# An attention and feed-forward kernel on one core: two PSUM banks joined wherever they lie, summary products on quadrants, a new table of due times, and identity matmuls ahead of the first chunk

## The chip, the core and the metric

One NeuronCore of a Trainium2 chip. Five engines work on separate instruction streams: PE (TensorE, matmuls; its weight loads are listed as PEld), DVE (VectorE), ACT (ScalarE), POOL (GpSimd) and SP, which here only issues DMAs. Matmuls write to PSUM, eight banks of 512 fp32 per partition; DVE and ACT read PSUM, and all but PE write SBUF. The metric is the device time of one execution in microseconds, the median of three runs.

## What is computed

```python
def mab(q, kv):                       # x: 4 x 12480 x 128, inducing: 32 x 128
    s = scale * (q @ kv.transpose(0, 2, 1))
    s = s - s.max(-1, keepdims=True)
    a = np.exp(s)
    a /= a.sum(-1, keepdims=True) + 1e-09
    return a @ kv
h = mab(I, x)                         # 32 summary rows for each batch
y = mab(x, h)                         # each row of x attends to them
g = where(y @ w_in >= 1, y @ w_in, where(y @ w_in <= -1, 0, (y @ w_in + 1) ** 2 / 4))
out = g @ w_out                       # w_in 128 x 2048, w_out 2048 x 128
```

## The kernel before

The four batches are cut into 26 chunks of 480 rows, 104 chunks in all. A batch has three stages. `summarize` reads x twice over (as rows and as columns), and makes the 32 summary rows h; a chain of small steps c1 to c12 joins its seven groups of four chunks and ends in hT, the transposed summary. `attend`, once for a group of four chunks, turns a chunk's scores against h into weights `a`, splits them into a high part `ahi` and a rest, and sends both by DMA into `aT`. `chunk` is the feed-forward part, and most of the time: since a chunk's attended rows are `a` times h, `y @ w_in` is `aT` times (h times w_in), and that summary product is kept for a batch in the four tiles `hw`, each with h times w_in four times over (two copies of the high part and two of the rest, to go with the four quarters of `aT`).

A chunk has eight steps k, each with two of the 16 blocks of 128 hidden columns. In a step:

- PE: two `hidden` matmuls (L774), each into a PSUM bank of its own, from a pool `h` of seven banks;
- ACT: relu of h + 1 out of PSUM into `w` (L782), then the square of half of it in place (L768);
- DVE: `bound`, min(square, max(h, 1)), out of PSUM and `w` (L787), which frees the banks;
- for six of eight steps (`SPLIT`) a high part `hi` is rounded off, on DVE (L810), ACT (L807) or POOL (L805), as the planner picks; POOL subtracts it (`lo`, L813); and PE adds three products into the chunk's accumulator bank (pool `o`, one bank): w_lo x hi, w_hi x hi, w_hi x lo (L844). In the two other steps PE multiplies `w` itself in full fp32 (L844, `w_f`);
- after eight steps DVE transposes the accumulator (L854), and SP stores it in four DMAs.

Relu and bound of a step are written as one instruction over both banks (128x960) where the second bank is the neighbour of the first and the pair starts on an even bank (`beside`, L83), and as two of 128x480 otherwise.

The order of everything is made ahead of time. `Plan.order` is a list scheduler: it goes through time with a cost and a lag for each operation, and at each moment an engine takes, of the operations whose inputs and buffers are there, the one with the earliest due time. Due times are a step's number times 1950 plus an offset by its kind (`BEHIND`), and offsets of the attention's steps (`STEPS`, `LEAD`, `SC`, `GA`). What it puts out is one fixed stream for each engine; on the chip an engine takes its stream strictly in that order.

The opening: the first summary needs all of batch 0, and the weights arrive as 64-bit numbers that DVE turns into fp32 in six to seven small instructions a tile. PE has no chunk work until hT, hw and the first `aT` are there.

Of the kernel before, what the change touches and what calls it, by code (L numbers as in the profile page):

```python
# [17 lines left out]
SPLIT = (0, 1, 3, 4, 6, 7)  # L18

SLOTS = dict(  # L20
    h=7, o=1, xn=9, xT=26, xr=2, e1=1, eN=1, hw=6, w=8, hi=4, lo=4, aT=3, s2=2, a=1, ahi=1, oT=1
# [3 lines left out]
BEHIND = {  # L25
    "h": -4400, "r": -3050, "s": -700, "t": 400, "hi": 3700, "hi ACT": 14900, "hi POOL": 9600,
    "lo": 2200, "p": 9300, "ps": 8900,
}

LEAD = 66950  # L30
STEPS = [0, 1200, 2400, 3600, 8000, 12000, 13000, 18000, 24000, 28000, 32000]

SC = [0, 1200, 2400]
GA = [0, 1500, 6000, 7500]


# [3 lines left out]

KEEP = 0


class Slot:


    def __init__(self, pool, turn=None, near=None):
        self.pool, self.left, self.until, self.place, self.tile = pool, 0, 0, None, None
        self.turn, self.near, self.first = turn, near, False
        if near:  # L50
            near.first = True

    def pick(self, spare, now):

        free = {i for t, i in spare if t <= now}
        if self.near and self.near.place is not None and self.near.place ^ 1 in free:
            return self.near.place ^ 1
        if self.first:
            return min(free, key=lambda i: (i ^ 1 not in free, i % 2, i))
        return min(free, key=lambda i: (i ^ 1 in free, i))  # L60


class Op:


    def __init__(self, engine, cost, lag, due, emit, needs, uses, tiled):
        choice = engine if isinstance(engine, dict) else {engine: (cost, lag, due)}
        self.choice, self.emit, self.uses = choice, emit, uses
        self.engine, self.cost, self.due = None, 0, due
        self.tiled, self.twin, self.merged, self.wide = tiled, None, None, False  # L70
        self.start = self.after = 0
        self.by = {}
        self.unmet, self.then = 0, []
        for n in needs:
            n.then.append(self)
            self.unmet += 1
        for s in self.uses:
            s.left += 1

    def ready(self, engine):  # L80
        return max([self.after, *(t for e, t in self.by.items() if e == engine)])

    def beside(self):  # L83

        a, b = self.uses[0].place, self.twin.uses[0].place
        return a % 2 == 0 and b == a + 1


class Plan:
# [5 lines left out]
    def add(self, engine, cost, lag, due, emit, needs=(), uses=(), tiled=False):  # L95
        op = Op(engine, cost, lag, due, emit, [n for n in needs if n], uses, tiled)
        self.ops.append(op)
        return op

    @staticmethod  # L100
    def twins(a, b, cost, lag):

        a.twin, b.twin, a.merged = b, a, (cost, lag)

    def order(self):
        engines = sorted({e for op in self.ops for e in op.choice})
        free = dict.fromkeys(engines, 0)
        able = {e: [] for e in engines}

# [3 lines left out]

        for op in self.ops:
            if not op.unmet:
                enable(op)
        spare = {p: [(0, i) for i in range(n)] for p, n in SLOTS.items()}
        turn = dict.fromkeys(SLOTS, 0)
        tiled = False
        now, done = 0, []  # L120
        while len(done) < len(self.ops):
            later = []
            took = False
            for e in engines:
# [3 lines left out]
                best, rank = None, 0  # L128
                for op in able[e]:
# [12 lines left out]
                    due = op.choice[e][2] - (KEEP if e == "PE" and op.tiled == tiled else 0)  # L142
                    if best is None or due < rank:
                        best, rank = op, due
# [6 lines left out]
                for s in best.uses:  # L151
                    if s.place is None:
                        s.place = s.pick(spare[s.pool], now)
# [10 lines left out]
                if e == "PE" and best.tiled != tiled:  # L164
                    cost, lag, tiled = cost + RETILE, lag + RETILE, best.tiled
                for op in both:
                    op.start, op.engine, op.cost, op.lag = now, e, 0, lag
                    done.append(op)
                best.cost = cost
                free[e] = now + cost  # L170
                later.append(free[e])
                for s in [s for op in both for s in op.uses]:
                    s.left -= 1
                    s.until = max(s.until, now + lag)
                    if not s.left:
                        spare[s.pool].append((s.until, s.place))
                for n in [n for op in both for n in op.then]:
                    n.unmet -= 1
                    if list(n.choice) == [e]:
                        n.after = max(n.after, now + cost + RAW[e])  # L180
                    elif e in n.choice:
                        for x in n.choice:
                            n.by[x] = max(n.by.get(x, 0), now + cost + RAW[e] if x == e else now + lag)
                    else:
                        n.after = max(n.after, now + lag)
                    if not n.unmet:
                        enable(n)
# [7 lines left out]
def attn_moe(  # L195
# [38 lines left out]
        xr=([C, NB, M], F32), e1=([P, CW], F32), eN=([96, 5, P], F32), hw=([P, 512], F32R),  # L234
# [23 lines left out]

    turns = dict.fromkeys(SLOTS, 0)

    def in_turn(pool, near=None):
        turns[pool] += 1
        return Slot(pool, turns[pool] - 1, near)
# [127 lines left out]
    def load_out(k, when, due):  # L391
        src = w_out[k * WS : (k + 1) * WS].rearrange("(p t) d -> p t d", t=2)
        if k not in SPLIT:
            w_f[k] = const.tile([P, 2, C], F32, name=f"w_f{k}")
            w_made[k] = load_f32(src, when, due, w_f[k])[0]
            return
        made, f = load_f32(src, when, due)
        w_hi[k] = const.tile([P, 2, C], F32R, name=f"w_hi{k}")
        w_lo[k] = const.tile([P, 2, C], F32R, name=f"w_lo{k}")
        by = lambda a: a.rearrange("p (t c) -> p t c", t=2)  # L400
# [5 lines left out]
        w_made[k] = add("POOL", 650, 750, due, lower, [made], [f])  # L406
# [6 lines left out]
    def summarize(b, begin, pace, end):  # L413
# [7 lines left out]
        def load(g, due, step):  # L421
            for q in range(nqs[g]):
# [6 lines left out]
                    "SP", 700 if b else 960, 3000, due,  # L429
# [20 lines left out]
                else:  # L450
# [6 lines left out]
                    def turn(c=c, xr=xr):  # L457
# [3 lines left out]
                        add("SP", 640, 3200, due - 4000, lambda k=k, fetch=fetch: fetch(k), [], [xr, xT[b, c]])  # L461
                        for k in range(Q)
                    ]
                    xT_made[b, c] = add("DVE", 597, 735, due, turn, l, [xT[b, c], xr])

        def score(g, due):
# [31 lines left out]
            m = add("PE", 850, 1050, due, scores, [ind_made, *(xT_made[b, c] for c in cs)],  # L498
                    [p1, e1[g], *(xT[b, c] for c in cs)], tiled=True)
            v = add("DVE", 760, 900, due + SC[1], most, [m, folded, prior], [p1])  # L500
            return add("ACT", 640, 780, due + SC[2], exps, [v], [e1[g], p1])

        def gather(g, due, scored):
# [32 lines left out]
            def keep():  # L536
                nc.scalar.copy(hs[:rows, g, :], ph.tile[:rows, :C])

            m = add("PE", 110 * T, 110 * T + 200, due, turn, [scored], [*to, e1[g], eN[g]])
            by = dict(ACT=(660, 800, due + GA[1])) if b == 0 else dict(  # L540
                DVE=(598, 740, due + GA[1]), ACT=(503, 640, due + GA[1]))
            v = add(by, 0, 0, 0, put, [m], [eN[g], *to])
            m = add("PE", 220 * T, 220 * T + 200, due + GA[2], weigh, [v],
                    [ph, eN[g], *(xn[g * Q + q] for q in range(nq))], tiled=True)
            lasts.append(add("ACT", 160, 300, due + GA[3], keep, [m, folded, prior], [ph]))
# [66 lines left out]
        def c12():  # L612
            hT[b] = const.tile([C, Q, M], F32, name=f"hT_{b}")
            nc.vector.tensor_copy(hT[b], s_h.tile[:, :M].unsqueeze(1).to_broadcast([C, Q, M]))
# [3 lines left out]
        o = add("DVE", 200, 350, end, c3, [o], [s_m])  # L618
# [8 lines left out]
        hT_made[b] = add("DVE", 180, 320, end, c12, [o], [s_h])  # L627
        hw[b], hw_made[b] = [], []
        for k in range(FF // 512):
            s_w, dst = Slot("h"), Slot("hw")  # L630
            hw[b].append(dst)

            def multiply(k=k, s_w=s_w):
                nc.tensor.matmul(  # L634
                    make(s_w), hT[b].rearrange("c q m -> c (q m)"),
                    w_in_sb[:, k * 512 : (k + 1) * 512], start=True, stop=True,
                )

            def upper(s_w=s_w, dst=dst):
                nc.scalar.copy(make(dst), s_w.tile)  # L640

            def lower(s_w=s_w, dst=dst):
                half = slice(P // 2, P)
                nc.vector.tensor_sub(dst.tile[half], s_w.tile[half], dst.tile[half].bitcast(F32))

            m = add("PE", 860, 1050, end + 1 + 2 * k, multiply, [hT_made[b], *in_made[2 * k : 2 * k + 2]], [s_w, dst])
            c = add("ACT", 485, 620, end + 1 + 2 * k, upper, [m], [dst, s_w])
            hw_made[b].append(add("DVE", 610, 745, end + 2 + 2 * k, lower, [c], [s_w, dst]))
# [4 lines left out]
    def attend(b, g, due):  # L653

        hasty = (b, g) == (0, 0)
        AT = [0] * 11 if hasty else STEPS
# [9 lines left out]
        def scores():  # L666
            p = make(p2)
            for q, c in enumerate(cs):
                nc.tensor.matmul(  # L669
                    p[q * M : (q + 1) * M, :CW], hT[b][:, 0, :], xT[b, c].tile, start=True, stop=True  # L670
# [43 lines left out]
        o = add("PE", 850, 1050, due, scores, [hT_made[b], *(xT_made[b, c] for c in cs)],  # L714
                [p2, p3, s2, *(xT[b, c] for c in cs)], tiled=True)
        o = add("DVE", 600, 740, due + AT[1], turn, [o], [p2, p3])
        o = add("DVE", 562, 700, due + AT[2], most, [o], [p3])
# [197 lines left out]
```

## Time and profile before

| what | us |
|---|---|
| runs, median (lowest to highest) | 1773.66 (1773.36 to 1774.67) |
| the profiled execution | 1771.55 |
| its span, first to last instruction | 1769.7 |
| busy: PE, ACT, DVE, POOL | 1717.7, 1695.4, 1622.8, 1610.4 |
| first `hidden` matmul | 72.06 |

The page gives busy times; groups of instructions by line and by shape give how many there are and how long one takes; the timeline gives starts, and from start to start, where an engine doesn't wait, the step of one. The step is shorter than the duration on PE and ACT, since the next instruction begins before the last has ended: a sum over durations counts too much, and a sum over steps is the load.

### The profile page before, as it was taken

The numbers are of one execution on the slowest core, as the hardware profiler recorded it, in microseconds if no ns is written. First come the engines' busy times: TensorE is split into PE (matmuls) and PEld (weight loads), VectorE is DVE, ScalarE is ACT, GpSimd is POOL, SyncE is SP. The second block draws the span as 40 slices with busy tenths as digits, with TensorE's granted clock in tenths as the row PEclk, the third lists the DMA queues.
The fourth block names the chain that finished last, engine by engine and source line by source line (L and its number), as shares of the span: only waits on it lengthen the run. The fifth ranks groups of instructions, "written<-read, shape, count | busy, mean of one in ns | idle before, by whom it ended". The sixth has DMA issues, their size and how long they took to land.

```text
span 1769.7 us, 26019 instructions
## 1 busy us (share of the span) xinstructions
PE 1717.7 (97%) x7898; PEld 1226.7 (69%) x7898; DVE 1622.8 (92%) x2393; ACT 1695.4 (96%) x2658; POOL 1610.4 (91%) x863
## 2 busy tenths in 40 slices
PE   7699999999999999999999999999999999999998
PEld 5467677777767677776767777677776777777676
DVE  7899889998899898999889999899889999999996
ACT  5599999999999999999999999999999999999997
POOL 0499999999899999999999999999998999999997
PEclk9699999999999999999999999999999999999999
DMA  9532423423232343332233423332211111111111
GB/s 243 98 63 56 79 49 60 72 58 60 44 67 49 62 79 59 65 76 48 47 56 61 72 49 64 70 65 51 45 20 38 34 27 30 35 34 34 33 29 17
DMA packets 425069, 101.78 MB, mean 58 GB/s; under 512 B 369602, under 2 KB 420386, under 8 KB 424930
## 3 DMA queue, kind: packets, MB, share of 16 engines
q1 hardware_dynamic: 424834, 100.01, 30.1%
q8 instruction: 62, 1.02, 0.2%
q14 instruction: 77, 0.63, 0.1%
q10 hardware_dynamic: 96, 0.12, 0.0%
HBM read 48.94 MB, written 25.56 MB: 42 GB/s over the span
## 4 chain that ended last, share of the span: by engine, by line
PE 49%; ACT 25%; DVE 13%; issue 7%; POOL 3%; DMA 2%; SPq 1%; DVEq 0%; POOLq 0%; ACTq 0%
PE banks L844 34%; ACT w L782 13%; PE banks L774 10%; ACT w L768 10%; DVE w L787 7%; DVE hi L810 3%; POOL lo L813 2%; ACT hi L807 1%; PE banks L669 1%; DVE oT L854 1%; PE banks L477 1%; PE banks L530 1%; PE banks L634 1%; SPq L455 1%; POOL hi L805 1%
## 5 line engine op out<-in xcount | busy, mean ns | idle before, releaser
L813 POOL TENSOR_TENSOR lo<-w,hi 128x960 fp32r<-128x960 f32 x624 | 1399.7, 2269 | 63.4 <-DVE hi L810 28.4
L787 DVE SCALAR_TENSOR_TENSOR w<-banks,w 128x480 f32<-128x480 f32 (+1 forms) x1428 | 978.0, 729 | 95.5 <-ACT w L768 85.3
L782 ACT ACTIVATE w<-banks 128x480 f32<-128x480 f32 (+1 forms) x1503 | 889.2, 666 | 12.3 <-PE banks L774 9.5
L768 ACT ACTIVATE w<-w 128x960 f32<-128x960 f32 x832 | 867.0, 1066 | 2.2
L774 PE MATMUL banks<-aT,hw 128*128 128x480 f32 x1664 | 594.9, 431 | 18.2 <-DVE w L787 9.9
L844 PE MATMUL banks<-hi,w_lo 128*128 128x480 f32 x1248 | 538.3, 431 | 9.5 <-DVE oT L854 5.7
L844 PE MATMUL banks<-lo,w_hi 128*128 128x480 f32 x1248 | 474.6, 380 | 1.4 <-POOL lo L813 1.4
L844 PE MATMUL banks<-hi,w_hi 128*128 128x480 f32 x1248 | 474.0, 380 | 0.0
L810 DVE TENSOR_REDUCE hi<-w 128x960 fp32r<-128x960 f32 x373 | 423.7, 1140 | 11.7 <-PE banks L844 0.9
L774 PEld LDWEIGHTS banks<-aT,hw 128*128 128x128 f32 x1664 | 306.7, 189 | 184.1 <-DVE w L787 107.1
L844 PE MATMUL banks<-w,w_f 128*128 128x480 f32 x832 | 393.1, 567 | 0.2 <-DVE oT L854 0.2
L844 PEld LDWEIGHTS banks<-hi,w_lo 128*128 128x128 f32 x1248 | 234.9, 188 | 119.9 <-issue 53.4
L844 PEld LDWEIGHTS banks<-hi,w_hi 128*128 128x128 f32 x1248 | 235.3, 189 | 57.6 <-issue 28.9
L844 PEld LDWEIGHTS banks<-lo,w_hi 128*128 128x128 f32 x1248 | 234.5, 188 | 39.6 <-POOL lo L813 2.9
L844 PEld LDWEIGHTS banks<-w,w_f 128*128 128x128 f32 x832 | 156.1, 189 | 62.6 <-issue 44.3
L805 POOL TENSOR_SCALAR hi<-w 128x960 fp32r<-128x960 f32 x145 | 144.4, 999 | 16.3 <-DVE w L787 9.7
L807 ACT CAST hi<-w 128x960 fp32r<-128x960 f32 x106 | 109.6, 1034 | 7.2 <-PE banks L844 3.3
L854 DVE STREAM_TRANSPOSE oT<-banks 128x480 f32<-128x480 f32 x104 | 70.1, 674 | 7.8 <-PE banks L844 7.5
L403 POOL TENSOR_TENSOR w_lo<-hi,w_hi 128x256 fp32r<-128x256 f32 x6 | 6.5, 1076 | 60.6 <-ACT w_hi L405 60.6
L458 DVE STREAM_TRANSPOSE xT<-xr 128x480 f32<-128x480 f32 x78 | 51.2, 663 | 3.1 <-DMA xr<-in_x 3.0
L712 POOL TENSOR_TENSOR a<-a,ahi 128x480 fp32r<-128x480 f32 (+1 forms) x27 | 33.2, 1231 | 1.3 <-ACT ahi L709 1.3
L530 PE MATMUL banks<-xn,eN 120*32 120x128 f32 (+1 forms) x774 | 31.7, 275 | 0.5 <-ACT eN L522 0.5
(82 smaller groups left out, 553.1 us busy)
## 6 DMA issues: line engine op xcount, KB each, us to landing
out<-oT SPq DMA_DIRECT2D x416, 60.0 KB, 2.2
xn<-in_x SPq DMA_DIRECT2D x93, 240.0 KB, 4.2
xr<-in_x SPq DMA_DIRECT2D x312, 60.0 KB, 2.5
aT<-ahi SPq DMA_DIRECT2D x208, 60.0 KB, 2.0
aT<-a SPq DMA_DIRECT2D x206, 60.0 KB, 2.0
w<-in_x SPq DMA_DIRECT2D x11, 240.0 KB, 4.5
w<-in_moe_w_in SPq DMA_DIRECT2D x8, 256.0 KB, 4.5
w<-in_moe_w_out SPq DMA_DIRECT2D x8, 256.0 KB, 5.3
```

The costliest lines, as they stand in the source:

```text
L458: nc.vector.transpose(make(xT[b, c]), xr.tile.rearrange("c n i -> c (n i)"))
L530: nc.tensor.matmul(p[q * M : (q + 1) * M, :C], eN[g].tile[:, t, q * M : (q + 1) * M], xn[g * Q + q].tile[:, t, :], start=(t == 0), stop=(t ...
L768: nc.scalar.activation(w.tile, w.tile, AF.Square, scale=0.5)
L774: nc.tensor.matmul(make(h)[:, :CW], hw[b][ft // 4].tile[:, ft % 4 * P : (ft % 4 + 1) * P], aT[b, c].tile, start=True, stop=True,)
L782: each(of, i, hs_, w, lambda to, h: nc.scalar.activation(to, h, AF.Relu, bias=1.0))
L787: lambda to, h: nc.vector.scalar_tensor_tensor(to, h, 1.0, to, op0=ALU.max, op1=ALU.min),
L805: nc.gpsimd.tensor_scalar(make(hi), w.tile, 1.0, 0.0, op0=ALU.mult, op1=ALU.add)
L807: nc.scalar.copy(make(hi), w.tile)
L810: nc.vector.tensor_reduce(make(hi), w.tile.unsqueeze(3), axis=AX.X, op=ALU.max)
L813: nc.gpsimd.tensor_sub(make(lo), w.tile, hi.tile.bitcast(F32))
L844: nc.tensor.matmul(acc.tile[:, :CW], wt, g, start=(first and n == 0), stop=(last and n == len(terms) - 1),)
L854: nc.vector.transpose(make(oT).rearrange("c n i -> c (n i)"), acc.tile[:, :CW])
```

## The change

**Joined banks.** `beside` and the rules that looked for neighbouring banks go. Any two banks of a step are read as one operand, with the distance between them as the stride; where the lower bank was taken second, the two halves of the step are swapped (`half`). Relu and bound are joined whenever both halves are ready at once.

**Summary products.** hT is kept once and not four times. The four products h times w_in go side by side into one bank, on the array's four quadrants of 32 columns; ACT rounds them once (`hx`), DVE subtracts once (`hy`), and SP copies 32-row pieces into the four `hw` tiles: 16 DMAs a batch, which weren't there.

**Three products in two parts.** w_lo x hi and w_hi x hi are one operation (`p`), which needs `hi` alone; w_hi x lo is another (`pl`), which needs `lo`.

**Due times.** `BEHIND`, `STEPS`, `LEAD`, `SC` and `GA` give way to a table `DUE` with an offset for each kind and each k. PE gains a bonus of 450 for staying in its mode of tiling, single halves a lateness (`LONE`), and a few costs change by some ns (hi on POOL from 1085 to 1000).

**Identity matmuls.** Up to 180 multiplications of the 128x128 identity by itself stand open to PE, one each 250 ns of the plan from 28 us on, behind everything else and dropped after 2 us; 111 get into the stream. They write the accumulator's bank, which the first chunk gets after them. The copy of the two fp32 weight tiles moves from DVE to ACT.

```diff
-    def beside(self):
-
-        a, b = self.uses[0].place, self.twin.uses[0].place
-        return a % 2 == 0 and b == a + 1
...
-                if best.merged and best.beside():
+                if best.merged:
...
+            a, b = sorted(h.place for h in hs_)
+            do(w.tile, banks[:, a : b + 1 : b - a, :CW])
...
+            for k in range(FF // 512):
+                nc.tensor.matmul(
+                    p[k * M : (k + 1) * M], hT[b], w_in_sb[:, k * 512 : (k + 1) * 512], start=True, stop=True
+                )
...
+                src = (wide_hi if r < 2 else wide_lo).tile[k * M : (k + 1) * M]
+                nc.sync.dma_start((dst.tile or make(dst))[r * M : (r + 1) * M].bitcast(F32), src.bitcast(F32))
...
+                parts = [
+                    ([(w_lo, hi), (w_hi, hi)], 436, "p", [u], [hi]),
+                    ([(w_hi, lo)], 218, "pl", [l], [lo]),
+                ]
...
-BEHIND = {
-    "h": -4400, "r": -3050, "s": -700, "t": 400, "hi": 3700, "hi ACT": 14900, "hi POOL": 9600,
+    "h": [-8100, -3450, -2750, -3300, -3950, 1600, -30300, -35450],
+    "r": [5450, 8600, 10700, -1550, 18200, -11550, -13450, -10800],
...
+    idle = Slot("o")
+
+    def keep_on():
+        nc.tensor.matmul((idle.tile or make(idle))[:, :P], ident, ident, start=True, stop=True)
+
+    for n in range(WARM[1]):
+        begin = WARM[0] + 250 * n
+        add("PE", 215, 415, -EARLY * 1e6 + n, keep_on, [id_made], [idle], span=(begin, begin + 2000))
```

How often each form stands in the streams, counted over all rows of the order:

| form | before | after |
|---|---|---|
| ACT relu, 128x480 / 128x960 | 1342 / 161 | 680 / 492 |
| DVE bound, 128x480 / 128x960 | 1192 / 236 | 0 / 832 |
| hi on DVE / ACT / POOL | 373 / 106 / 145 | 416 / 74 / 134 |
| summary product: PE / ACT / DVE / SP | 16 / 16 / 16 / 0 | 16 (four at once) / 4 / 4 / 64 |
| eN copies of 120 rows: DVE / ACT | 11 / 10 | 4 / 17 |
| identity matmuls | 0 | 111 |

First place: PE between the summary and the first chunk. L634 (before) is a summary product, L669 a chunk's scores against h, L774 a `hidden` matmul. Before:

```order
L634 MATMUL banks<-w_in_sb,hT_906 128x512 x4
L669 MATMUL banks<-xT_298,hT_906 32x480
L669 MATMUL banks<-xT_311,hT_906 32x480
L669 MATMUL banks<-xT_321,hT_906 32x480
L669 MATMUL banks<-xT_359,hT_906 32x480
L669 MATMUL banks<-xT_387,hT_906 32x480
L669 MATMUL banks<-xT_403,hT_906 32x480
L669 MATMUL banks<-xT_413,hT_906 32x480
L669 MATMUL banks<-xT_432,hT_906 32x480
L774 MATMUL banks<-aT_973,hw_925 128x480 x4
```

And now (L654 the product, L701 the scores, L903 the identity, L811 a `hidden` matmul):

```order
L654 MATMUL banks<-w_in_sb,hT_946 32x512 x4
L701 MATMUL banks<-xT_298,hT_946 32x480
L701 MATMUL banks<-xT_311,hT_946 32x480
L701 MATMUL banks<-xT_321,hT_946 32x480
L701 MATMUL banks<-xT_359,hT_946 32x480
L903 MATMUL banks<-ident 128x128 x27
L701 MATMUL banks<-xT_387,hT_946 32x480
L701 MATMUL banks<-xT_403,hT_946 32x480
L701 MATMUL banks<-xT_413,hT_946 32x480
L701 MATMUL banks<-xT_432,hT_946 32x480
L903 MATMUL banks<-ident 128x128 x17
L811 MATMUL banks<-aT_1047,hw_983 128x480 x4
```

Of the 111 identity matmuls 44 stand here, 40 ahead of it among c1 to c12 and the last groups, and 27 between the first chunk's `hidden` matmuls.

Second place: DVE near the end, L787 and L824 the bound, L810 and L847 hi. Before:

```order
L787 SCALAR_TENSOR_TENSOR w_16671<-banks,w_16671 128x480 x2
L787 SCALAR_TENSOR_TENSOR w_16685<-banks,w_16685 128x960
L810 TENSOR_REDUCE hi_16733<-w_16671 128x960
L787 SCALAR_TENSOR_TENSOR w_16700<-banks,w_16700 128x480 x2
L787 SCALAR_TENSOR_TENSOR w_16720<-banks,w_16720 128x480 x2
```

And now:

```order
L824 SCALAR_TENSOR_TENSOR w_15974<-banks,w_15974 128x960
L847 TENSOR_REDUCE hi_16000<-w_15950 128x960
L824 SCALAR_TENSOR_TENSOR w_15979<-banks,w_15979 128x960
L847 TENSOR_REDUCE hi_16021<-w_15979 128x960
L824 SCALAR_TENSOR_TENSOR w_15993<-banks,w_15993 128x960
```

Every bound is one instruction. Third place: PE in a middle chunk, L844 and L876 the products into the accumulator. Before:

```order
L844 MATMUL banks<-hi_7621,w_lo_101 128x480
L844 MATMUL banks<-hi_7621,w_hi_100 128x480
L844 MATMUL banks<-lo_7638,w_hi_100 128x480
L844 MATMUL banks<-hi_7621,w_lo_101 128x480
L844 MATMUL banks<-hi_7621,w_hi_100 128x480
L844 MATMUL banks<-lo_7638,w_hi_100 128x480
L774 MATMUL banks<-aT_7264,hw_4985 128x480 x4
```

And now:

```order
L876 MATMUL banks<-hi_7853,w_lo_91 128x480
L876 MATMUL banks<-hi_7853,w_hi_90 128x480
L876 MATMUL banks<-hi_7853,w_lo_91 128x480
L876 MATMUL banks<-hi_7853,w_hi_90 128x480
L811 MATMUL banks<-aT_7503,hw_4875 128x480
L876 MATMUL banks<-lo_7884,w_hi_90 128x480 x2
```

The products with `lo` come after those with `hi`, and `hidden` matmuls stand between them. At the three later changes of batch the summary product stands 20 to 24 `hidden` matmuls ahead of the first that needs it (before: 16).

More of the change, by code (lines that the diff above doesn't have):

```diff
@@ L108, in order @@
         able = {e: [] for e in engines}
+        spare = {p: [(0, i) for i in range(n)] for p, n in SLOTS.items()}
+        turn = dict.fromkeys(SLOTS, 0)
+        tiled = False
+        now, done, left = 0, [], len(self.ops)
         def enable(op):
@@ L116, in order @@
                 enable(op)
[L117 to L121, printed above, removed]
+        while left:
             later = []
@@ L168, in order @@
                     done.append(op)
+                    left -= 1
+                    finish(op, e, cost, lag)
                 best.cost = cost
[L170 to L187, printed above, removed]
             if not took:
```

285 lines of the change are left out of this document (152 added, 133 removed), and 15 rows, old and new, of the table DUE.

## The prediction

> **What bounds the kernel now.** I read the page's busy times first, then a table of windows, then groups of instructions by shape, and last the timeline of three engines for their steps. A difference of 0.2% (3.5 us) is about what a measurement of this kernel can tell from none. The page, and the engines' busy time in a quiet stretch (length, then PE, PEld, DVE, ACT, POOL in us with counts, PE's granted clock, DMA):
>
> ```profile
> PE 1717.7 (97%) x7898; PEld 1226.7 (69%) x7898; DVE 1622.8 (92%) x2393; ACT 1695.4 (96%) x2658; POOL 1610.4 (91%) x863
> 300.00:400.00 100.00, 99.43 (x473) 71.72 (x472) 94.18 (x141) 99.86 (x161) 96.29 (x51) 1.00 0.34 63
> ```
>
> Four engines are nearly full at once, so the question is whose load is largest. Busy time overstates it for ACT and PE, whose instructions overlap, so I count instructions and multiply by steps, start to start. The groups (count, busy us and mean ns, idle before):
>
> ```profile
> L813 POOL TENSOR_TENSOR lo<-w,hi 128x960 fp32r<-128x960 f32 x624 | 1399.7, 2269 | 63.4 <-DVE hi L810 28.4 <-ACT hi L807 8.5 <-PE banks L844 7.4
> L768 ACT ACTIVATE w<-w 128x960 f32<-128x960 f32 x832 | 867.0, 1066 | 2.2
> L782 ACT ACTIVATE w<-banks 128x480 f32<-128x480 f32 x1342 | 733.4, 626 | 11.5 <-PE banks L774 8.7 <-DMA aT<-a 1.2
> L787 DVE SCALAR_TENSOR_TENSOR w<-banks,w 128x480 f32<-128x480 f32 x1192 | 713.9, 645 | 45.2 <-ACT w L768 41.7 <-POOL lo L813 1.7
> L810 DVE TENSOR_REDUCE hi<-w 128x960 fp32r<-128x960 f32 x373 | 423.7, 1140 | 11.7 <-PE banks L844 0.9 <-POOL hi L805 0.5
> L787 DVE SCALAR_TENSOR_TENSOR w<-banks,w 128x960 f32<-128x960 f32 x236 | 269.2, 1149 | 50.3 <-ACT w L768 43.6 <-issue 3.8 <-POOL hi L805 1.6
> L782 ACT ACTIVATE w<-banks 128x960 f32<-128x960 f32 x161 | 160.8, 1002 | 0.8 <-PE banks L774 0.8
> L805 POOL TENSOR_SCALAR hi<-w 128x960 fp32r<-128x960 f32 x145 | 144.4, 999 | 16.3 <-DVE w L787 9.7 <-PE banks L844 1.3 <-DVE sm L698 1.1
> L807 ACT CAST hi<-w 128x960 fp32r<-128x960 f32 x106 | 109.6, 1034 | 7.2 <-PE banks L844 3.3 <-DVE w L787 2.7 <-DVE nm L585 0.6
> L644 DVE TENSOR_TENSOR hw<-banks,hw 64x512 fp32r<-64x512 f32 x16 | 10.9, 693 | 3.7 <-ACT hw L640 3.3
> ```
>
> Steps on ACT (start, duration, row), all without a wait:
>
> ```profile
> 1743.73 0.99 ACT L782 ACTIVATE w<-banks 128x960 f32<-128x960 f32 x1
> 1744.58 1.02 ACT L807 CAST hi<-w 128x960 fp32r<-128x960 f32 x1
> 1745.46 1.07 ACT L782 ACTIVATE w<-banks 128x480 f32<-128x480 f32 x2
> 1746.37 1.05 ACT L768 ACTIVATE w<-w 128x960 f32<-128x960 f32 x1
> 1747.27 1.07 ACT L782 ACTIVATE w<-banks 128x480 f32<-128x480 f32 x2
> ```
>
> A joined relu takes 0.85 us, a pair of single ones 0.91, a cast 0.88, a square 0.90. On DVE:
>
> ```profile
> 1717.71 1.14 DVE L810 TENSOR_REDUCE hi<-w 128x960 fp32r<-128x960 f32 x1
> 1718.77 1.15 DVE L787 SCALAR_TENSOR_TENSOR w<-banks,w 128x960 f32<-128x960 f32 x1
> 1719.83 0.67 DVE L854 STREAM_TRANSPOSE oT<-banks 128x480 f32<-128x480 f32 x1
> 1720.43 1.19 DVE L787 SCALAR_TENSOR_TENSOR w<-banks,w 128x480 f32<-128x480 f32 x2
> 1721.53 1.14 DVE L810 TENSOR_REDUCE hi<-w 128x960 fp32r<-128x960 f32 x1
> ```
>
> Joined bound 1.06, pair 1.10, hi 1.06. On PE, an fp32r matmul steps (1760.86 - 1758.91) / 9 = 0.217 us over the rows below, and the two full fp32 ones (four records) take 1758.91 - 0.22 - 1757.09 = 1.60, so 0.80 each:
>
> ```profile
> 1757.09 1.77 PE L844 MATMUL banks<-w,w_f 128*128 128x480 f32 x4
> 1758.32 0.75 PE L844 MATMUL banks<-hi,w_lo 128*128 128x480 f32 x1
> 1758.91 0.38 PE L844 MATMUL banks<-hi,w_hi 128*128 128x480 f32 x1
> ...
> 1760.86 0.38 PE L844 MATMUL banks<-hi,w_hi 128*128 128x480 f32 x1
> ```
>
> Loads in the chunk stage, which I take from the first `hidden` matmul at 72.06 (quoted below) to the end of the span, 1769.7, so 1698 us. ACT: 671 pairs x 0.91 + 161 x 0.85 + 832 x 0.90 + 106 x 0.88 = 1590, and some 55 of attention steps, an estimate from four kinds of 21 to 28 of about half a us: 1645, or 96.9% of the stage. PE: 1664 + 3 x 1248 = 5408 matmuls x 0.217 = 1173, 416 x 0.80 = 333, some 104 of attention and summary, an estimate: 1610, 94.8%. POOL: 1610 busy, of which an estimated 9 lie before the stage: 1601, 94.3%. DVE: 596 pairs x 1.10 + 236 x 1.06 + 373 x 1.06 = 1301, and some 224 of transposes and attention, an estimate: 1525, 90%. So ACT is the bound, by a small lead, and the waits agree:
>
> ```profile
> ACT w L782 <- PE banks L774: 9.5, 17, 1.5
> DVE w L787 <- ACT w L768: 85.3, 124, 2.9
> PE banks L774 <- DVE w L787: 9.9, 21, 1.4
> ```
>
> DVE waits for ACT's square, ACT hardly for anyone.
>
> **The change: ACT.** By the counts in the order, 331 steps more have a joined relu: 331 x (0.91 - 0.85) = 20 us less. 32 casts go: 32 x 0.88 = 28 less. Nine summary casts fewer and seven eN copies more cancel. ACT: 1645 - 48 = 1597. No row shows a pair of banks that are not neighbours. If its access costs as two singles, the 20 us stay; that it costs less than neighbours I exclude, as it is the same form with a longer stride. I take the neighbours' 0.85, the nearest row.
>
> **DVE, POOL, PE.** DVE: 596 more joined bounds x 0.04 = 24 less, 43 more hi x 1.06 = 46 more, 9 summary subtractions and 7 copies of about 0.6 less, 10: 1525 + 12 = 1537, still the lightest. POOL: 11 hi of 1.0 less: 1590. PE: 12 products in the stage are about 0.86 each when the clock is full (512/480 of 0.80); three joint ones replace them. On quadrants the nearest rows are the scores (0.85 for four, below); dearer than 0.9 or cheaper than 0.8 moves the sum by 0.3 us. So 7.6 less: 1602. Cutting the products with `lo` apart adds no matmul. It takes PE's wait for POOL off the products with `hi`, which I cost at nothing: the waits that PE shows there come to a few us.
>
> The largest load falls from 1645 to 1602, and now three engines lie within 12 us of each other. If the top one keeps nearly the share that ACT has, 96.7% for 96.9, the stage takes 1602 / 0.967 = 1657: **41 us less**.
>
> **The 64 new DMAs.** The nearest rows are the aT load's, from SP too (the page's, with the us to landing, and two issues in the timeline):
>
> ```profile
> aT<-ahi SPq DMA_DIRECT2D x208, 60.0 KB, 2.0
> 72.24 1.22 SPq L733 DMA_DIRECT2D aT<-ahi  x2
> ```
>
> Sixteen at a change of batch, at about 0.6 us of issue, are 10 us, and 2.0 to land. Behind them on SP stand aT loads and stores. In the order the product stands 20 to 24 `hidden` matmuls ahead of its first use, that is 1.25 chunks or more, and a chunk takes 1698 / 104 = 16 us: 20 us cover 13. If that cover is gone, it costs up to 10 us at each of three changes. I take nothing.
>
> **The opening.** The clock (column after the five engines) and PE's rows:
>
> ```profile
> 50.00:53.00 3.00, 0.71 (x4) 0.62 (x3) 2.88 (x13) 0.67 (x2) 0.38 (x2) 0.50 1.14 222
> 53.00:56.00 3.00, 3.00 (x14) 2.94 (x14) 2.17 (x7) 0.00 (x0) 0.75 (x1) 0.50 0.84 122
> 68.00:70.00 2.00, 0.00 (x0) 0.00 (x0) 1.98 (x4) 0.44 (x1) 0.00 (x0) 0.81 0.12 30
> 52.88 3.20 PE L610 MATMUL banks<-ff,hs 128*128 128x32 f32 x14 [1.13 <-DVE ff L602]
> 56.46 1.83 PE L669 MATMUL banks<-xT,hT 128*32 128x480 f32 x8 [0.38 <-DVE hT L614]
> 58.22 5.78 PE L634 MATMUL banks<-w_in_sb,hT 128*128 128x512 f32 x8
> 63.93 1.01 PE L669 MATMUL banks<-xT,hT 128*32 128x480 f32 x8
> 72.06 1.17 PE L774 MATMUL banks<-aT,hw 128*128 128x480 f32 x2 [5.09 <-DMA aT<-a]
> ```
>
> At half clock the same scores take 1.83 us that take 1.01 at full. With the clock held, c11 (L610) saves 3.20 x (1 - 1.01 / 1.83) = 1.4 and the first scores 0.8. On DVE one summary subtraction stands between the scores and aT where three of 0.69 did: 1.4. The identity matmuls, 0.80 x 128/480 = 0.21 us each, an estimate from the fp32 step, hide in PE's waits; the six or seven ahead of c4, c8 and c11 fill those waits a little more than full, 0.4 late in all. 27 + 17 between the scores are 9.4 us beside the chain of some 12 on DVE. Together 3.2 us earlier. After 72 ACT was full anyway, so a warm clock there is worth nothing more.
>
> By the Trainium skill's page "TensorE: Matmul & The Clock Gate", Part 1, the clock is full again after about 3.4 us of sustained work. The trace doesn't bear that out here: PE worked from 52.88 with hardly a gap and the scores at 56.46, 3.6 us on, still ran at half. By the page c11 would save nothing in its last part, and the sum would be 1 us smaller at most.
>
> **The sum.** 1771.55 - 41 - 3.2 = 1727, for the profiled execution; the median of the runs is 2.1 higher: **1729 us**.
>
> **Rivals.**
>
> *The mean share stays, not the top one.* With three equal loads somebody is always late. The four loads sum to 6381 before and 6326 after; at the same mean share the stage shrinks by 0.9%, 15 us: 1771.55 - 15 - 3.2 + 2.1 = 1755. For it: any wait stops two engines now. Against: `pl` apart from `p` and every bound in one piece loosen PE.
>
> *The clock falls all the same.* It was at 0.50 from 50 to 53, with four small matmuls and 0.71 us of work in 3. If the identities are too thin to hold it, each takes 0.43, and the 44 hold up the third scores and the first chunk: 5.5 us of work, 44 x 0.43 = 19, 1.8 more, so first `hidden` at about 56 + 26 = 82 and not 72. That gives 1771.55 - 41 + 10 + 2.1 = 1743. Against: they stand back to back.
>
> *Banks become the bound: slower.* A joined bound holds the first bank one half longer, 0.55 us: 596 x 0.55 = 328 us of bank time, over seven banks 47 us of the stage, if PE always waits for a bank. Then the gain on ACT isn't felt either: 1771.55 + 47 - 3.2 + 2.1 = 1817. It decides for slower when it binds over half of the program, as (41 + 3.2) / (41 + 47) = 0.50. For it: the row of PE's waits names the bound as releaser. Against: that is 9.9 us of 1698.
>
> **How the numbers follow.** Forecast 0.55 (its own range 1700, a top share of about 98.5%, to 1742, joined relus that cost like single ones), mean share 0.23, cold clock 0.08, banks 0.14. The range takes the first three, with 7 us for the changes of batch on the mean share's 1755: 1700 to 1762. Faster: the first three, 0.86. Banks split at their point of balance: same 0.04, slower 0.10.
>
> **What would show it.** Right: 832 joined bounds at about 1.06 a step and 492 joined relus at 0.85; ACT, PE and POOL each at 96 to 97% of a stage of some 1657 us; clock 1.00 from 44 to 85 and the first `hidden` at about 69. Mean share: the same loads with more idle time on all four, and waits of ACT for PE well over 9.5. Cold: 0.50 in the clock column near 60. Banks: PE's wait for the bound grows from 9.9 to over 45. The forecast is wrong if joined forms over distant banks cost more than the pair, or if the first chunk of a batch waits for `hw`.

## The result and the profile after

The kernel got slower by a third: 2378.97 us, median of runs from 2372.31 to 2386.57, against 1773.61 (1773.36 to 1774.67) for the kernel before; the ratio is 1.341, interval 1.337 to 1.346. The profiled execution of after has a span of 2379.2 us, 609.5 more than before's.

The page of after, busy times and the chain that ended last, by engine and by line:

```profile
PE 1917.3 (81%) x8120; PEld 1282.1 (54%) x8120; DVE 1668.3 (70%) x1821; ACT 1717.4 (72%) x2292; POOL 1598.6 (67%) x852
...
DVE 31%; ACT 30%; PE 27%; issue 6%; POOL 2%; SPq 1%; DMA 1%; DVEq 0%; ACTq 0%; POOLq 0%
DVE w L824 27%; ACT w L819 20%; PE banks L876 14%; PE banks L811 10%; ACT w L805 8%; DVE hi L847 2%; POOL lo L850 1%; PE banks L549 1%; PE banks L496 1%; PE banks L701 1%; DMA xn<-in_x 1%; SPq L674 1%; DVE oT L888 0%; ACT hi L844 0%; DVE banks L707 0%
```

POOL's busy time is 12 us less than before, ACT's 22 more, DVE's 46 more; nothing there makes 609.5 us. PE's 200 more come with a lower granted clock (0.953, for 0.991 before), and PE holds only 27% of the chain. No engine is the bound any more: the chain goes to and fro between three.

Groups of instructions by shape in after (count, busy us and mean ns, then, behind the second bar, idle time before them and its releasers):

```profile
L824 DVE SCALAR_TENSOR_TENSOR w<-banks,w 128x960 f32<-128x960 f32 x832 | 954.7, 1154 | 609.7 <-ACT w L819 339.9 <-PE banks L811 132.9 <-ACT w L805 101.0
...
L819 ACT ACTIVATE w<-banks 128x960 f32<-128x960 f32 x492 | 475.2, 972 | 327.1 <-DVE w L824 229.8 <-PE banks L811 75.1 <-PE banks L876 6.3
...
L819 ACT ACTIVATE w<-banks 128x480 f32<-128x480 f32 x680 | 373.9, 570 | 236.7 <-DVE w L824 144.7 <-PE banks L811 88.2 <-POOL lo L850 1.5
```

A joined bound takes 1154 ns (1149 before), a joined relu 972 (1002 before): reading two banks that lie apart is hardly slower than reading neighbours. Most of what was lost stands behind the second bar: 609.7 us before the bounds and 563.8 before the relus, where before had 95.5 and 12.3, joined and single together. The releasers are odd, too: a relu (L819) needs its own two `hidden` tiles from PE and a free `w`, yet what it waits for most is DVE's bound. The waits in after (us in total, times, longest; the rows of weight loads, PEld, are left out):

```profile
ACT w L819 <- DVE w L824: 374.6, 333, 3.9
DVE w L824 <- ACT w L819: 339.9, 318, 3.8
PE banks L811 <- DVE w L824: 274.7, 277, 3.1
...
PE banks L811 <- ACT w L819: 131.5, 124, 2.9
```

Before had 9.9 us for the third and no row for the other three. `hidden` matmuls (L811) waiting for a relu is new in kind: no relu frees a bank.

**Which banks.** The plan of after says which PSUM banks each tile has, and the instructions of the trace can be counted off against it. 2 us of the timeline of after, with the wait before each in brackets:

```profile
901.91 0.38 PE L811 MATMUL banks<-aT,hw 128*128 128x480 f32 x1
...
902.40 1.16 DVE L824 SCALAR_TENSOR_TENSOR w<-banks,w 128x960 f32<-128x960 f32 x1 [1.98 <-PE banks L811]
...
903.65 1.44 ACT L819 ACTIVATE w<-banks 128x960 f32<-128x960 f32 x2 [0.78 <-DVE w L824]
904.65 1.16 DVE L824 SCALAR_TENSOR_TENSOR w<-banks,w 128x960 f32<-128x960 f32 x1 [1.10 <-ACT w L819]
...
904.67 0.48 PE L811 MATMUL banks<-aT,hw 128*128 128x480 f32 x1 [0.58 <-ACT w L819]
```

| start | instruction | its banks | waited for | whose banks |
|---|---|---|---|---|
| 902.40 | bound 302 | 0, 3 | `hidden` 609 | 2 |
| 903.65 | relu 427, first of the row's two | 1, 6 | bound 302 | 0, 3 |
| 904.65 | bound 303 | 4, 5 | relu 427 | 1, 6 |
| 904.67 | `hidden` 611 | 3 | relu 427 | 1, 6 |

No two instructions of a row share a bank. But in each row a bank of one lies between the two banks of the other. The streams carry these waits: the order of after has them on the same instructions as semaphores (relu 427 stands there as `L819 ACTIVATE w_6746<-banks 128x960 [waits DVE_49,Pool_49]`, where a relu of the kernel before mostly waits for PE alone). Over the whole program of after, 412 relus wait by semaphore for a bound, 420 bounds for a relu and 222 `hidden` for a relu with which they share no bank; in before these are 2, 0 and 0. So the order is already in the program when it reaches the chip. The theory, called reach below: **an instruction that is written over banks a and b with the stride b - a is kept in order with everything on all banks from a to b.** By the plan 397 of the 492 joined relus and 681 of the 832 joined bounds have other banks between their two. They reach over 1044 and 1779 banks, counted once for each instruction.

The rivals: the access itself is slow (the durations above speak against it), the longer hold of a bank by a joined bound (the prediction's slower rival), and the four new parts crowding each other.

### The profile page after: what moved, and what is told of

It reads as the page before. It is cut to its first block, busy times and chain, and to the rows that moved or that the text cites. A ratio compares the mean times of both kernels' runs of the same rounds, so it can differ in the third digit from the quotient of the medians.

```text
span 2379.2 us, 25695 instructions
## 1 busy us (share of the span) xinstructions
PE 1917.3 (81%) x8120; PEld 1282.1 (54%) x8120; DVE 1668.3 (70%) x1821; ACT 1717.4 (72%) x2292; POOL 1598.6 (67%) x852
## 4 chain that ended last, share of the span: by engine, by line
DVE 31%; ACT 30%; PE 27%; issue 6%; POOL 2%; SPq 1%; DMA 1%; DVEq 0%; ACTq 0%; POOLq 0%
DVE w L824 27%; ACT w L819 20%; PE banks L876 14%; PE banks L811 10%; ACT w L805 8%; DVE hi L847 2%; POOL lo L850 1%; PE banks L549 1%; PE banks L496 1%; PE banks L701 1%; DMA xn<-in_x 1%; SPq L674 1%; DVE oT L888 0%; ACT hi L844 0%; DVE banks L707 0%
## 5 line engine op out<-in xcount | busy, mean ns | idle before, releaser
L824 DVE SCALAR_TENSOR_TENSOR w<-banks,w 128x960 f32<-128x960 f32 x832 | 954.7, 1154 | 609.7 <-ACT w L819 339.9
L819 ACT ACTIVATE w<-banks 128x480 f32<-128x480 f32 (+1 forms) x1172 | 837.3, 739 | 563.9 <-DVE w L824 374.6
L811 PE MATMUL banks<-aT,hw 128*128 128x480 f32 x1664 | 669.0, 459 | 416.3 <-DVE w L824 274.7
L805 ACT ACTIVATE w<-w 128x960 f32<-128x960 f32 x832 | 814.8, 1004 | 3.1
L811 PEld LDWEIGHTS banks<-aT,hw 128*128 128x128 f32 x1664 | 308.3, 196 | 749.2 <-DVE w L824 457.9
L876 PE MATMUL banks<-hi,w_lo 128*128 128x480 f32 x1248 | 515.7, 413 | 4.7 <-DVE oT L888 4.1
L876 PE MATMUL banks<-hi,w_hi 128*128 128x480 f32 x1248 | 494.6, 396 | 0.0
L847 DVE TENSOR_REDUCE hi<-w 128x960 fp32r<-128x960 f32 x416 | 473.0, 1142 | 22.0 <-PE banks L876 8.0
L876 PE MATMUL banks<-lo,w_hi 128*128 128x480 f32 x1248 | 416.3, 408 | 0.5 <-POOL lo L850 0.5
L876 PE MATMUL banks<-w,w_f 128*128 128x480 f32 x832 | 407.6, 590 | 0.0
L876 PEld LDWEIGHTS banks<-hi,w_lo 128*128 128x128 f32 x1248 | 248.3, 199 | 69.8 <-issue 21.9
L876 PEld LDWEIGHTS banks<-lo,w_hi 128*128 128x128 f32 x1248 | 245.9, 199 | 71.8 <-issue 33.0
L876 PEld LDWEIGHTS banks<-hi,w_hi 128*128 128x128 f32 x1248 | 248.5, 199 | 47.5 <-issue 9.3
L876 PEld LDWEIGHTS banks<-w,w_f 128*128 128x128 f32 x832 | 163.3, 197 | 66.5 <-issue 49.0
L844 ACT CAST hi<-w 128x960 fp32r<-128x960 f32 x74 | 73.4, 992 | 15.2 <-DVE w L824 14.4
L733 POOL TENSOR_TENSOR s<-s,sm 128x480 f32<-128x480 f32 (+1 forms) x27 | 26.9, 998 | 20.1 <-DVE sm L730 18.5
```

What stands on the lines that cost most here:

```text
L805: nc.scalar.activation(w.tile, w.tile, AF.Square, scale=0.5)
L811: nc.tensor.matmul(make(h)[:, :CW], hw[b][ft // 4].tile[:, ft % 4 * P : (ft % 4 + 1) * P], aT[b, c].tile, start=True, stop=True,)
L819: each(of, i, hs_, w, lambda to, h: nc.scalar.activation(to, h, AF.Relu, bias=1.0))
L824: lambda to, h: nc.vector.scalar_tensor_tensor(to, h, 1.0, to, op0=ALU.max, op1=ALU.min),
L844: nc.scalar.copy(make(hi), w.tile)
L847: nc.vector.tensor_reduce(make(hi), w.tile.unsqueeze(3), axis=AX.X, op=ALU.max)
```

## The experiments

All ratios are to the kernel before on the same chip. Line numbers differ a little from kernel to kernel.

**1. After's own order, pairs over distant banks in two pieces.** Nothing is moved; only how such a relu or bound is written changes.

```diff
-        if of[i].wide:
-            a, b = sorted(h.place for h in hs_)
+        a, b = sorted(h.place for h in hs_)
+        if of[i].wide and b - a > 1:
+            for j in range(2):
+                do(w.tile[:, half(j, hs_)], hs_[j].tile[:, :CW])
+        elif of[i].wide:
```

> The changed kernel in its own order, but a joined relu or bound whose two banks are not neighbours is written as two instructions of 128x480, one for each bank. Reach theory (a joined instruction is kept in order against everything on all banks from its lower to its upper one; 681 of 832 joined bounds and 397 of 492 joined relus reach over other banks): those waits go, ACT's relu waits for DVE's bound fall from 374.6 us to under 20, and the time to 1735 to 1775. Crowding theory (four equal loads in an order tuned to a model): order and loads are nearly the same, so it stays above 2250. Bank-hold theory (joined bounds free the first bank late): 681 x 0.55 us over seven banks come back, 54 us, so about 2325.

1751.11 us (1750.53 to 1751.63), ratio 0.988 (0.986 to 0.989). 628 us come back, 22 more than the change had lost, so the kernel beats the one before. Its page, and its waits (L822 the relu, L827 the bound, L814 `hidden`):

```profile
PE 1718.9 (98%) x8120; PEld 1237.9 (71%) x8120; DVE 1654.7 (95%) x2502; ACT 1675.8 (96%) x2689; POOL 1598.5 (91%) x852
```

```profile
ACT w L822 <- PE banks L814: 10.3, 19, 1.5
...
PE banks L814 <- DVE w L827: 5.7, 14, 0.8
```

The relu's wait for the bound is gone, and of the semaphores counted above 12, 0 and 0 are left. Crowding falls: products in two parts, quadrants, DMAs, due times and identities are all still there.

**2. The kernel before, its pairs moved apart.** Same streams, same 397 joined instructions (161 relus and 236 bounds); the seven banks are only renumbered, so that each pair has two banks between.

```diff
+APART = (0, 3, 1, 4, 2, 5, 6)
...
-            slot.tile = banks[:, slot.place + (SLOTS["h"] if slot.pool == "o" else 0), :]
+            slot.tile = banks[:, APART[slot.place] if slot.pool == "h" else SLOTS["h"], :]
...
-            do(w.tile, banks[:, hs_[0].place : hs_[0].place + 2, :CW])
+            a = APART[hs_[0].place]
+            do(w.tile, banks[:, a : a + 4 : 3, :CW])
```

> The kernel before in its own order, every instruction the same, but the seven banks of the pool are renumbered (0,3,1,4,2,5,6), so that its 161 joined relus and 236 joined bounds take banks that lie three apart and reach over two others. Reach theory: the waits of the changed kernel come up here too; 397 reaching instructions of 1078 there cost in proportion to the 605 us, some 220, and since fewer are near each other perhaps half: 1880 to 2000. Crowding and bank-hold theories: nothing that they speak of has moved, so 1768 to 1779.

1948.67 us (1946.33 to 1951.18), ratio 1.099 (1.097 to 1.101): as reach had it. The instruction that frees each bank is the same as in before, so the longer hold can't be the cause here. Its waits (L786 relu, L791 bound, L778 `hidden`) are of after's kind, on a kernel that has no other part of the change:

```profile
DVE w L791 <- ACT w L786: 113.8, 112, 3.8
PE banks L778 <- DVE w L791: 95.2, 108, 2.4
...
ACT w L786 <- DVE w L791: 73.9, 83, 2.3
```

**3. The same with one bank between**, by `APART = (0, 2, 1, 3, 4, 6, 5)` and a stride of 2.

> The kernel before, its own streams, with the pool's banks renumbered so that the two banks of its 161 joined relus and 236 joined bounds lie two apart, with one bank between them (three apart, with two banks between, took 1949 us, 175 more than before). Reach theory (a joined instruction is kept in order with everything on the banks between its two): one bank between instead of two, so about half of the 175: 1835 to 1905 us. Rival, any pair that is not of neighbours costs, whatever lies between: again about 1949 us (1925 to 1970). Rival, nothing but a long distance costs: 1773 to 1790 us.

1848.96 us (1848.27 to 1850.63), ratio 1.043 (1.041 to 1.045). The loss is 76 us where two banks between cost 175: it goes with the number of banks reached over, not with being apart as such.

**4 and 5. Which half of the pairs.** As the first experiment (the diff is against its kernel), with only the relus split, then with only the bounds split.

```diff
-        if of[i].wide and b - a > 1:
+        if of[i].wide and b - a > 1 and split:
```

> After's own order; only the relus over banks that are not neighbours are written as two instructions; the bounds stay joined at any distance. Reach theory, the loss shared out by the number of instructions that reach over other banks (681 bounds, 397 relus, of 628 us together): the bounds alone keep 63% of it, some 400 us: 2050 to 2250 us. Rival, it takes both (an ACT and a DVE instruction that reach over each other's banks): the relus split give back nearly all, under 1880 us. Rival, the relus alone matter, since ACT is the fullest engine: under 1800 us.

> After's own order; only the bounds over banks that are not neighbours are written as two instructions; the relus stay joined at any distance. Reach theory, by the number of reaching instructions: the relus alone keep 37% of 628 us, some 230: 1900 to 2080 us. Rival, it takes both forms: under 1880 us, as with the relus split. Rival, the relus alone matter: over 2300 us.

Relus split: 2167.68 us (2164.49 to 2168.48), ratio 1.222 (1.220 to 1.224). Bounds split: 1977.44 (1974.51 to 1978.54), ratio 1.115 (1.113 to 1.117). Over 1751 the bounds alone cost 417 us and the relus alone 226, together 643 for the 628 of both: they add to within 15 us. Divided by the banks reached over:

| kernel | loss, us | banks reached over | us for each |
|---|---|---|---|
| before, pairs two apart | 76 | 397 | 0.19 |
| before, pairs three apart | 175 | 794 | 0.22 |
| after, only bounds reach | 417 | 1779 | 0.23 |
| after, only relus reach | 226 | 1044 | 0.22 |
| after, both | 628 | 2823 | 0.22 |

Five kernels between 0.19 and 0.23 us. That is a fit for this kernel, with all engines near full, and no law.

**6. The planner joins neighbours only**, in whichever order they were taken.

```diff
+    def beside(self):
+        a, b = self.uses[0].place, self.twin.uses[0].place
+        return None not in (a, b) and abs(a - b) == 1
...
+                        and op.beside()
...
-                if best.merged:
+                if best.merged and best.beside():
```

> The changed kernel, planned so that only neighbouring banks are joined, in either order of the two (197 joined relus, 295 joined bounds; hi on DVE, ACT, POOL 387, 91, the rest). Due times, identity matmuls, quadrant products and parted products stay. Reach theory: no reaching left, 1735 to 1775. Crowding theory: the due times are the same, so above 2250.

1758.26 us (1757.65 to 1758.65), ratio 0.992 (0.990 to 0.993); 197 joined relus and 295 joined bounds.

**7. The planner also picks a neighbour** for the second half, where one is free.

```diff
+    def pick(self, spare, now):
...
+        beside = lambda i: {i - 1, i + 1}
+        if self.near and self.near.place is not None:
+            got = beside(self.near.place) & free
+            if got:
+                return min(got, key=lambda i: (len(beside(i) & all_), i))
...
```

> As the kernel with neighbours only, but the planner picks for the second bank of a step a neighbour of the first where one is free (335 joined relus, 493 joined bounds). Reach theory: ACT and DVE have a little less to do than with 197 and 295, so 1725 to 1765, no slower than that one. Crowding theory: above 2250.

1751.59 us (1750.2 to 1752.49), ratio 0.988 (0.987 to 0.989). 335 joined relus and 493 joined bounds without a wait that belongs to reach:

```profile
L847 DVE SCALAR_TENSOR_TENSOR w<-banks,w 128x960 f32<-128x960 f32 x493 | 557.1, 1145 | 54.6 <-ACT w L828 47.6 <-issue 3.4 <-POOL lo L873 1.6
L842 ACT ACTIVATE w<-banks 128x960 f32<-128x960 f32 x335 | 326.8, 989 | 0.7 <-PE banks L834 0.6
```

**8. Distant pairs joined, but only over idle banks.** As 7, but the planner joins any two banks when by its own times nothing is under way on those between, and holds those back meanwhile. Against the kernel of 7:

```diff
+            return None not in (a, b) and all(last[i] <= now for i in range(min(a, b) + 1, max(a, b)))
...
-                if best.merged and best.beside():
+                if best.merged and joins(best, now):
...
```

> The kernel with picked neighbours, where the planner may join distant banks too if nothing is under way on the banks between, and holds those banks back until the joined instruction has ended (372 joined relus, 597 joined bounds). If reach over the banks between is all that a distant pair costs, ACT has 6 us less to do: 1742 to 1750. If a distant pair costs more than that, above 1756.

1769.52 us (1766.85 to 1771.48), ratio 0.997 (0.996 to 0.998): 18 us slower than 7, a miss. 372 joined relus and 597 joined bounds, as long as ever (992 and 1145 ns), so the dearer access isn't what did it. The waits of reach are back, small (L854 relu, L859 bound, L846 `hidden`), and the first `hidden` comes at 75.94 and not 72.51:

```profile
ACT w L854 <- DVE w L859: 10.8, 20, 1.0
...
DVE w L859 <- ACT w L854: 8.1, 16, 1.2
...
PE banks L846 <- DVE w L859: 14.8, 30, 1.5
```

The plan's idle bank is not always idle on the chip. How the 18 us divide between these waits, the later start and the holding back was not tried.

**9. Without the identities.** As 7, same order, the 111 multiplications left out.

> The kernel with picked neighbours in the same order, with the 111 identity matmuls left out. By the opening's terms in the prediction (c11 1.4, first scores 0.8, less 0.4 for the matmuls themselves) the first chunk starts 2 to 3 us later, so 1753 to 1755, with the clock at 0.50 from about 50 on. Rival: the first chunk itself at half clock holds up all the others, until PE is warm again some 11 us later, 1757 to 1762. Second rival: the start is hidden behind the attention chain on DVE, no change.

1755.72 us (1754.41 to 1757.24), ratio 0.989 (0.987 to 0.991): some 4 us slower by the medians, though the intervals of the ratios overlap. It lies between the first answer's range and the rival's, so it decides for neither. The windows (length, the five engines, granted clock) and two of PE's rows with the identities, in 7:

```profile
50.00:53.00 3.00, 3.00 (x31) 2.66 (x25) 2.75 (x10) 0.97 (x3) 1.02 (x1) 1.00 1.10 226
80.00:84.00 4.00, 4.00 (x25) 3.61 (x24) 3.40 (x5) 4.00 (x6) 3.86 (x3) 1.00 0.52 95
...
56.59 1.65 PE L651 MATMUL banks<-ff,hs 128*128 128x32 f32 x14
...
72.51 1.77 PE L834 MATMUL banks<-aT,hw 128*128 128x480 f32 x7
```

And without them:

```profile
50.00:53.00 3.00, 0.95 (x3) 0.57 (x3) 2.91 (x11) 0.88 (x3) 1.37 (x1) 0.50 1.13 224
80.00:84.00 4.00, 2.27 (x6) 1.92 (x7) 2.70 (x4) 4.00 (x7) 4.00 (x3) 0.51 0.52 92
...
55.12 3.20 PE L651 MATMUL banks<-ff,hs 128*128 128x32 f32 x14 [1.13 <-DVE ff L643]
...
73.08 2.34 PE L834 MATMUL banks<-aT,hw 128*128 128x480 f32 x5 [8.86 <-DMA aT<-a]
```

They do hold the clock: with them it is 1.00 in every window from 47 to 100 us, without them 0.50 from 50 to 62. c11 (L651) takes 1.65 us for 3.20, but starts 1.5 later with identities ahead of the small products before it; so the first `hidden` gains only 0.6. The rest of the 4 us, if it is there, comes after 72: without them the first chunk starts at half clock (0.50 from 72 to 76), and 80 to 84 has 0.51 again.

**10 to 12. One part undone, and planned anew.** Each is 7 with one thing as it was before the change: four full summary products without the DMAs; the old due times (with neither bonus nor lateness); the three products in one piece. The last as a diff:

```diff
-                    ([(w_lo, hi), (w_hi, hi)], 436, "p", [u], [hi]),
-                    ([(w_hi, lo)], 218, "pl", [l], [lo]),
+                    ([(w_lo, hi), (w_hi, hi), (w_hi, lo)], 654, "pl", [l], [hi, lo]),
```

> The kernel with picked neighbours, planned anew, with the old summary products: four full ones of PE, four casts of ACT and four subtractions of DVE a batch, no DMAs for hw. By loads PE gains 7.6 us in the chunk stage and ACT about 4, and DVE's subtractions stand in the opening again (1.4): 1755 to 1762. Rival: the 64 DMAs and the longer path at a change of batch cost as much as the products, 1746 to 1753.

> The kernel with picked neighbours, with the due times of the kernel before put into the table (one offset for all k, no bonus for staying in a tiling mode, no lateness of single halves). By loads: ACT has 1034 single and 315 joined relus and 113 casts, 17 us more than with the new table, so 1765 to 1772. If the new due times are worth more than what they move between engines, 1775 or more; if the whole gain over the kernel before comes from the other parts, 1748 to 1755.

> The change with joins of neighbouring banks alone and a planner that picks a neighbour for the second half (1751.6 us), replanned with the three products in one piece again, as before the change. By the loads nothing changes on any engine; PE waits for POOL's lo once more ahead of products that need hi alone. If parting is worth what the prediction cost it at, nothing but the tightness of the plan: 1749 to 1762 us. If parting carries a good part of the gain: 1763 to 1780 us.

1771.85 us (1771.37 to 1775.64), ratio 0.999 (0.998 to 1.000); 1765.14 (1763.24 to 1766.44), ratio 0.994 (0.992 to 0.996); 1765.55 (1763.78 to 1768.25), ratio 0.996 (0.995 to 0.997). The first, at 20 us over 7, was a miss; the due times came out as expected, at the lower edge; the products fell to the answer that their parting carries a good part of the gain. But none of them measures its part alone, since each edit changes the whole plan: with full products there are 308 joined relus where 7 has 335. What is safe is that each of the three, together with what it does to the plan, is worth 14 to 20 us on top of the others; the three can't be added, since 7 as a whole is only 22 us faster than before.

## Why the prediction was wrong, point by point

**The price of a joined instruction: the step that failed.** "No row shows a pair of banks that are not neighbours ... I take the neighbours' 0.85, the nearest row." The duration held: 972 ns, and 1154 for the bound. What failed is that the step priced a joined instruction by its duration alone and put at nothing what it is kept in order with. An access over neighbours touches no third bank, so no row of before could show the cost. The bound from above, "as two singles", was no bound either: by experiment 1 the 2823 banks reached over cost 628 us. The prediction did name the place where it would be wrong, joined forms dearer over distant banks, but expected to see that on the instruction; it is on the instructions that wait.

The Trainium skill's page "PSUM — Partial Sum Buffer", section "PSUM bank collisions raise a hardware error", asks for a semaphore guard by bank and quadrant, not by address. By that rule none of the four waits in the table above is needed. The streams here do have them, and experiments 1 to 5 show what they cost.

**Banks as the bound.** The rival that came out slower had the right sign by luck, and its test was met: 9.9 us became 274.7. Its mechanism is wrong. It priced the longer hold of a bank at 47 us at most; moving the pairs of before apart changes no hold and costs 175, and 493 joined bounds on neighbours leave PE's wait for them at 6.6 us, less than before's:

```profile
PE banks L834 <- DVE w L847: 6.6, 18, 0.9
```

A rival's test that is met shows the place, not the cause.

**Loads and shares.** With reach taken away, the sum by steps holds. Experiment 1 has 1474 single relus and 95 joined ones: 737 x 0.91 + 95 x 0.85 + 832 x 0.90 + 74 x 0.88 + 55 = 1620 us on ACT, in a stage from 71.42 to 1749.6, 1678 us: 96.6%, where the prediction took 96.7. For 7 it is 497 x 0.91 + 335 x 0.85 + 832 x 0.90 + 94 x 0.88 + 55 = 1624 of 1678, 96.8%. So three engines with nearly equal loads don't make each other late here, against the mean-share rival; that its 1755 is near these results is chance, since it counts the joined relus' 20 us as had. What was missing from 1727 is the load: ACT stayed the bound at 1620 and 1624 us, where the prediction had 1597 and PE on top with 1602. In 1 the relus in two pieces cost 24 us more than joined ones; in 7 half of the 20 us is had, but it has 20 casts more than after, which take 18. Where waits of reach remain, in 8, ACT's share is lower: 460 x 0.91 + 372 x 0.85 + 832 x 0.90 + 90 x 0.88 + 55 = 1618 of 1694, 95.5%.

**The opening.** The clock was held, as forecast (1.00 in every window of after from 47 to 90 us), and the cold rival falls. The first `hidden` did not come at 69 but at 71.95; PE's rows in after:

```profile
56.03 1.65 PE L629 MATMUL banks<-ff,hs 128*128 128x32 f32 x14
58.36 1.01 PE L701 MATMUL banks<-xT,hT 128*32 128x480 f32 x8
59.19 1.04 PE L654 MATMUL banks<-w_in_sb,hT 128*32 128x512 f32 x8
60.04 0.99 PE L701 MATMUL banks<-xT,hT 128*32 128x480 f32 x8
...
71.95 1.78 PE L811 MATMUL banks<-aT,hw 128*128 128x480 f32 x7
```

c11 and the scores were as short as worked out. But c11 began at 56.03, 3.15 later than before. By experiment 9 the identities make some 1.5 of that, where the prediction had 0.4; the other half was not taken apart. The step "a warm clock there is worth nothing more" is doubtful too, by the same run, though its 4 us are not clear of noise.

**Quadrants and DMAs.** Four joint products take 0.85 us to the next row, as priced (59.19 to 60.04 in after). PE's waits for the 64 DMAs come to 0.5 us in after, and none shows in experiments 1 and 7. That the edit was worth only its 7.6 us on PE is doubtful by experiment 10, and what it is worth alone stays open. Parting the products, priced at nothing, was worth about 14 with its plan.

**What stays open**: how 8 loses its 18 us, what the three parts of 10 to 12 are worth on a plan of their own, and the other half of c11's delay. No version ran that gets all 492 joined relus without reach. The best are 1 and 7, 1.2% faster than before.

## What to carry to other kernels

When two tiles are read as one strided operand, ask what lies between them: the program's semaphores can keep the whole stretch in order, and the cost then shows as waits of other instructions and not in the duration of the one that was changed. Count the instructions that reach over others' buffers before pricing the join, and let the planner place the halves side by side instead of joining them where they fell. In the waits, look for releasers that no data flow explains, a relu waiting for a later step's bound, a matmul for a relu; they point to an order that nobody asked for.

## What was not expected of the hardware

A read of two banks up to six apart by DVE or ACT takes about as long as one of neighbours: on the mean 1154 ns for a joined bound in after and 1154 with all pairs three apart, 1149 in before; 972, 975 and 1002 for the relu. And the clock goes with the pauses of PE: in after's order (experiments 1, 5 and 4, then after itself) PE is busy for 98, 91, 85 and 81% of the span, and the granted clock is 1.000, 0.996, 0.981 and 0.953. From 300 to 400 us after is granted 0.95, with PE busy for 83 of 100 us, where before had 1.00:

```profile
300.00:400.00 100.00, 83.05 (x367) 56.08 (x365) 67.92 (x70) 76.53 (x103) 70.35 (x38) 0.95 0.28 53
```
